# A planned attention order: transfers that share a modelled wire, late tables and weights, half of k loaded, k cast by GpSimd

## The chip, the cores and the metric

The kernel runs on one core of one Trainium2 chip. The metric is the time of one execution on the device in microseconds (us); lower is better. The engines are TensorE (PE; its weight loads are listed as PEld), VectorE (DVE), ScalarE (ACT), GpSimd (POOL) and SyncE (SP, which here only issues transfers).

## What is computed

An attention with 4 x 8 heads of 576 x 64, whose scores carry a bias from a running sum of `s`, and behind it two expert layers over its 2304 rows of 512: a max of three products with an output product, and a routed layer with 8 experts, one chosen per row.

```python
scores = scale * np.matmul(q, k.transpose(0, 1, 3, 2))
cum = np.cumsum(np.maximum(s, 0.0), axis=-1)
bias = -(cum[:, :, :, None] - cum[:, :, None, :])
scores = np.where(causal, -1000000000.0, scores + np.minimum(bias, 0.0))
attn = softmax(scores); x = attn @ v                  # per head
h = np.maximum(np.maximum(x @ w1, x @ w2), x @ w3)    # first layer
x = h @ w_out
e_idx = np.argmax(x @ w_gate + modality_bias[modality_id], axis=1)
out[mask] = gate_w[mask, None] * (np.maximum(x[mask] @ w1[e], 0.0) @ w2[e])
```

## The kernel before

The 32 heads go in 16 pairs; the four pairs of a batch complete its rows of x. Every product is made in float32 out of rounded halves: a high part (`hl`, `xh`, `w_h`) and a low rest (`q_b`, `xl`, `w_l`).

Per head: `load_x` (L338) brings q and k, each held twice over 2 x 64 partitions, as one tile `qk_r` of 128 x 2 x 576. `k_high` (ck, L366) and `q_high` (cq, L369) cast to the high part `hl` on ACT, `k_low` (kl, L376) makes k's rest on DVE, `q_low` (ql, L379) q's rest `q_b` on POOL, and `k_again` (kb, L372) casts k into `k_b` on POOL. Two further rows of `k_b` hold the bias; they come by a transfer from `augk` (first pair, L352) or from `dk` in DRAM (L354). Then six times two matmuls for the scores (L386, L387), six minima on DVE that also write the scores to `e` (L395), five exponentials on ACT (L402), 15 transposes on PE (L407), and their copies to `pt` by ACT or DVE (L412).

Per pair: the sums `r` (ACT L416), their reciprocal (DVE L419), a transpose (PE L423), a copy `r_t` (ACT L427), a transfer to DRAM (`r_d`, SP L430) and two back, spread over 64 partitions each (`rb`, SP L435); the P·V matmuls (L442); and x = P·V times `rb` on DVE (L448, L452). DVE takes its instructions in order, so a late `rb` holds up all that stands behind L448.

Beside the heads run "fills": matmuls of the first expert layer (L240 to L242, 128 x 288, 504 of them) for rows whose pairs are done. They have the lowest priority on PE. Their weights come as 64-bit numbers (`w_raw`, 512 KB, SP L204), are turned by ACT and three DVE steps on `w_z`, sent by a POOL-issued transfer into `w_h` (L225), and POOL makes `w_l` (L229) when that has landed. Nine weight tiles go this way; the other fifteen are converted after the attention, by ACT and DVE.

All of this is one list of jobs (L489 to L550). `planned` (L112) walks through them with a cost per job, a landing time per transfer (`land`), a ring of buffers per kind (`BUFS`) and per engine one queue. At each step it takes, among the jobs that can start soon, the one with the lowest key (`KEY`, per kind, plus `T` for every head). The order so found is the program order of every engine, SP's queue included. Every transfer on SP also waits until the one eight transfers before it has landed. After the attention the order is the framework's.

Of the kernel before, what the change touches and what calls it, by code (L numbers as in the profile page):

```python
# [16 lines left out]
T = B * S  # L17
# [76 lines left out]
class Slot:  # L94

    def __init__(self, pool):
        self.pool, self.users = pool, []


class Job:  # L100

    def __init__(self, run, eng, ns, key, after=(), takes=(), uses=(), land=0, lock=False, ready=0, lag=0):
        self.run, self.eng, self.ns, self.key, self.ready = run, eng, ns, key, ready
        self.after, self.takes, self.land, self.lock, self.lag = list(after), list(takes), land, lock, lag
        self.start = self.end = self.done = None
        for u in [*uses, *takes]:
            if self not in u.users:
                u.users.append(self)


def planned(jobs):
    free, order, then, left, cand = {e: 0 for e in LAT}, {p: [] for p in BUFS}, {}, {}, {e: [] for e in LAT}  # L112
    lock_v = lock_g = 0
    out = []

    def behind(j, a):
        if a.eng == "SP" or a.eng != j.eng:
# [22 lines left out]
    while len(out) < len(jobs):  # L140
# [32 lines left out]
def fused_kernel(tc, qk, vd, sd, w64, mod, wg, wgt, mb, we, cst, csi, out):  # L173
# [3 lines left out]
    with top:  # L177
# [73 lines left out]
        with ExitStack() as es:  # L251
# [237 lines left out]
            for n, h in CONV:  # L489
                raw, z = Slot("raw"), Slot("z")  # L490
                a = job(("wl", n), lambda n=n: w_load(n), "SP", 450, at(h, "wl"), takes=[raw], land=W_NS)
                for k, (what, eng, ns, u, lock, land) in enumerate([("wz", "ACT", 669, [raw], False, 0), ("w1", "DVE", 424, [], False, 0), ("w1", "DVE", 686, [raw], True, 0), ("w1", "DVE", 690, [raw], True, 0), ("wd", "POOL", 570, [], False, 4000), ("ws", "POOL", 1277, [], False, 0)]):
                    a = job(("w", n), lambda n=n, k=k: w_step(n, k), eng, ns, at(h, what, k), after=[a], takes=[z] if k == 0 else [], uses=u + [z], land=land, lock=lock)
            rows = job("rows", rows_out, "SP", 1300, -1e8, ready=8700)
            turns = None
            for h in range(2 * NP):
                p, j = divmod(h, 2)
                s_x, s_k, s_h, s_q, s_e = (Slot(n) for n in ("qk", "kb", "hl", "qb", "e"))
                lx = job(("lx", h), lambda h=h: load_x(h), "SP", (1200, 900, 600)[min(h, 2)], at(h, "lx") if h > 2 else -1e9 + h, takes=[s_x], land=(3400, 3000, X_NS)[min(h, 2)], ready=750)
                lk = job(("lk", h), lambda h=h: load_k(h), "SP", 300 if h > 1 else 450, at(h, "lx", 1) if h > 1 else -2e8 + h, after=[rows] if h > 1 else [], takes=[s_k], land=2000, ready=7800)  # L500
# [21 lines left out]
                if j:  # L522
# [11 lines left out]
                if h % H == H - 1 and NFILL[b]:  # L534
                    for i in range(b * S // FW, (b + 1) * S // FW):
# [501 lines left out]
```

## Time and profile before

| | |
|---|---|
| time, median of 3 runs (lowest, highest) | 761.88 us (756.9, 762.68) |
| the profiled execution: time, span | 761.99 us, 760.2 us |
| PE busy | 715.9 us, 94% |
| PEld busy | 638.2 us, 84% |
| DVE busy | 518.5 us, 68% |
| ACT busy | 407.5 us, 54% |
| POOL busy | 180.9 us, 24% |
| transfers | 108.56 MB, 143 GB/s in the mean |

Busy time is a share over stages with different limits, and a busy PE is not PE at its peak, because the ends of its pipelined matmuls are modelled; the spacing of their starts tells its real pace. The attention takes about the first 242 us of the span, the expert layers the rest. [...] A row's bracket names the idle time of the engine in front of the instruction and what seems to have ended it.

### The profile page before, as it was taken

To read this page: it belongs to the slowest core of one execution; us is meant where nothing else is said; L and a number is where in the kernel's file an instruction comes from. 1 tells how busy PE (TensorE), PEld (TensorE's weight loads), DVE (VectorE), ACT (ScalarE), POOL (GpSimd) and SP (SyncE) were. 2 spreads that over 40 slices of the span, in tenths; PEclk is the share of its full clock that TensorE was granted. 3 is DMA by queue.
4 is the path that set the end of the run, shared out by engine and by line. 5 is a ranking of instruction groups with operands and counts; after the bars stand their busy time and mean duration, and the time that the engine had idled before them with its cause. 6 is when DMAs were issued, how large, how long until landed. Compare 5 with 4: busy or idle time off the path is not lost. (4 is left out here: it accounts for less than half of the span.)

```text
span 760.2 us, 13607 instructions
## 1 busy us (share of the span) xinstructions
PE 715.9 (94%) x4602; PEld 638.2 (84%) x4602; DVE 518.5 (68%) x1567; ACT 407.5 (54%) x992; POOL 180.9 (24%) x202
## 2 busy tenths in 40 slices
PE   1969889999999989999999999998999999999996
PEld 1757678778888989999898998997899888999884
DVE  4869987979777694294676876673786555576540
ACT  5869778887985352221222222444557555575541
POOL 5345645442430220001010101024133122121101
PEclk9989999999999999999999999999999999999999
DMA  6556775754432650011101012567587675756610
GB/s 218 194 162 192 234 207 147 236 147 156 146 88 71 217 168 36 11 43 10 55 10 63 22 48 22 183 192 193 146 196 289 218 241 191 262 209 196 208 68 18
DMA packets 45104, 108.56 MB, mean 143 GB/s; under 512 B 8992, under 2 KB 12992, under 8 KB 45024
## 3 DMA queue, kind: packets, MB, share of 16 engines
q1 hardware_dynamic: 37376, 90.75, 38.7%
q0 software_dynamic: 4912, 11.82, 5.4%
q10 hardware_dynamic: 2736, 5.01, 1.8%
q8 instruction: 38, 0.62, 0.4%
q14 instruction: 42, 0.34, 0.2%
HBM read 93.55 MB, written 12.18 MB: 139 GB/s over the span
## 5 line engine op out<-in xcount | busy, mean ns | idle before, releaser
L240 PE MATMUL a_ps<-xh,w_h 128*128 128x384 f32 (+2 forms) x492 | 160.5, 327 | 3.3 <-ACT h L482 2.2
L241 PE MATMUL a_ps<-xl,w_h 128*128 128x384 f32 (+2 forms) x492 | 157.5, 320 | 1.0 <-POOL xl L471 1.0
L242 PE MATMUL a_ps<-xh,w_l 128*128 128x384 f32 (+2 forms) x492 | 157.3, 320 | 0.2 <-POOL w_l L229 0.2
L739 DVE TENSOR_TENSOR e_l<-e_raw,e_h 128x512 fp32r<-128x512 f32 x160 | 104.2, 686 | 17.6 <-ACT e_h L738 15.9
L738 ACT CAST e_h<-e_raw 128x512 fp32r<-128x512 f32 x160 | 93.3, 622 | 20.2 <-DMA e_raw<-in_we 11.7
L240 PEld LDWEIGHTS a_ps<-xh,w_h 128*128 128x128 f32 x492 | 92.9, 189 | 4.9 <-ACT h L482 2.8
L402 ACT ACTIVATE e<-e,mn 128x448 f32<-128x448 f32 (+4 forms) x160 | 88.7, 556 | 12.2 <-DVE mn L395 12.1
L241 PEld LDWEIGHTS a_ps<-xl,w_h 128*128 128x128 f32 x492 | 93.0, 189 | 2.0 <-POOL xl L471 1.5
L242 PEld LDWEIGHTS a_ps<-xh,w_l 128*128 128x128 f32 x492 | 92.8, 189 | 0.5 <-POOL w_l L229 0.4
L769 PE MATMUL h_ps<-x2t,e_h 128*128 128x256 f32 x288 | 81.0, 282 | 0.0
L770 PE MATMUL h_ps<-x2t,e_l 128*128 128x256 f32 x288 | 80.9, 282 | 0.0
L768 PE MATMUL h_ps<-x2t,e_h 128*128 128x256 f32 x288 | 80.5, 282 | 0.0
L647 POOL DMA_INDIRECT table<-meta,si x18 | 19.7, 1093 | 248.5 <-DVE nm L635 70.5
L407 PE MATMUL t_ps<-ident,e 128*128 128x128 f32 x480 | 73.1, 285 | 5.5 <-DVE x L452 3.2
L622 DVE CUSTOM_DVE_ANT_0 junk<-x,wg 128x512 bf16<-128x512 f32 x96 | 65.9, 686 | 17.2 <-ACT x L700 16.2
L386 PE MATMUL s_ps<-hl 128*128 128x288 f32 (+1 forms) x192 | 64.9, 348 | 12.4 <-DVE hl L376 10.2
L395 DVE CUSTOM_DVE_ANT_0 e<-s_ps,mask 128x288 f32<-128x288 f32 (+4 forms) x160 | 63.7, 425 | 10.5 <-PE s_ps L387 9.9
L407 PEld LDWEIGHTS t_ps<-ident,e 128*128 128x128 f32 x480 | 55.8, 144 | 11.4 <-DVE x L452 4.3
L387 PE MATMUL s_ps<-k_b,q_b 66*128 66x288 f32 (+1 forms) x192 | 58.5, 318 | 5.3 <-POOL q_b L379 5.3
L798 PE MATMUL y_ps<-e_h,gh 128*128 128x512 f32 x152 | 61.5, 405 | 0.4 <-ACT gh L790 0.4
L800 PE MATMUL y_ps<-e_h,gl 128*128 128x512 f32 x152 | 60.7, 399 | 0.0
L799 PE MATMUL y_ps<-e_l,gh 128*128 128x512 f32 x152 | 60.0, 395 | 0.0
(177 smaller groups left out, 1466.1 us busy)
## 6 DMA issues: line engine op xcount, KB each, us to landing
e_raw<-in_we SPq DMA_DIRECT2D x80, 512.0 KB
qk_r<-in_qk SPq DMA_DIRECT2D x30, 576.0 KB
w_raw<-in_w SPq DMA_DIRECT2D x24, 512.0 KB
v_r<-in_vd SPq DMA_DIRECT2D x16, 320.0 KB
rb<-r_d SPq DMA_DIRECT2D x32, 160.0 KB
x2d<-x ACTq DMA_DIRECT2D x18, 256.0 KB
w_h<-w_z POOLq DMA_DIRECT2D x9, 256.0 KB, 7.2
wg<-in_wg SPq DMA_DIRECT2D x4, 512.0 KB
```

The source lines that it names most:

```text
L240: P.matmul(a_ps, wh[:, c], xh[:, c], start=c == 0, stop=False)
L241: P.matmul(a_ps, wh[:, c], xl[:, c], start=False, stop=False)
L242: P.matmul(a_ps, wl[:, c], xh[:, c], start=False, stop=c == 3)
L386: P.matmul(s_ps, hl[:, 1, q0:q0 + 128], hl[:, 0, k0:k0 + n], start=True, stop=False)
L402: A.activation(out=ec, in_=ec, func=ACTF.Exp, bias=tl["mn", h][:, c:c + 1], scale=-1.0, accum_out=tl["l", p][:, j, c:c + 1])
L407: P.transpose(out=t_ps[:, n * 128:(n + 1) * 128], in_=e_bufs[h % E_N][:, EOFF[c] + kb * 128:EOFF[c] + (kb + 1) * 128], identity=ident)
L622: V.tensor_tensor_reduce(out=junk, in0=x2, in1=wg_sb[ei // 2][:, ei % 2, :], scale=1.0, scalar=0.0, op0=ALU.mult, op1=ALU.add, accum_out=l ...
L738: A.copy(out=h, in_=raw[:, a])
L739: V.tensor_tensor(out=lo, in0=raw[:, a], in1=h.bitcast(F32), op=ALU.subtract)
L768: P.matmul(h_ps, w(hs, f, c), xt[:, 0, c], start=c == 0, stop=False)
L769: P.matmul(h_ps, w(hs, f, c), xt[:, 1, c], start=False, stop=False)
L770: P.matmul(h_ps, w(ls, f, c), xt[:, 0, c], start=False, stop=c == 3)
```

## The change

`CK` moves the cast of k's high part from ACT to POOL. `load_x` loads of k only partitions 64 to 127 (144 KB instead of 288) and q apart (288 KB), so two issues a head; `k_again` reads k from there. The planner gets a `wire`: transfers take their bytes' time one behind the other, 1.3 us after their issue at the earliest, and land 0.9 us later; before, each landed by a time of its own. The transfers of the tables for the routing may not start before 150 us of the plan, the weights' not before 15 us, and the landing of `w_h` is put at 3.5 us instead of 4.0. All numbers of `KEY` are new. The work of the engines is otherwise the same.

```diff
-CK = "ACT"
+CK = "POOL"
-W_NS, X_NS, SET_H = 6500, 4500, 24
-KEY = {"T": 6784, "wl": 43955, "wz": 15084, "w1": -2025, ...}
+W_READY, SET_H = 15000, 24
+WIRE_FROM, WIRE_TO, WIRE_SLOW = 1300, 900, 1.0
+KEY = {"T": 6868, "wl": 10316, "wz": -156821, "w1": 25206, ...}
...
-        return a.end + a.land + j.lag
+        return (a.done if a.wire or a.land else a.end) + j.lag
...
         j.done = j.end + j.land + TAIL.get(j.eng, 0)
+        if j.wire:
+            wire = max(wire, t + WIRE_FROM) + j.wire * WIRE_SLOW
+            j.done = max(j.done, wire + WIRE_TO)
...
-                if p == 0:
-                    for t in range(2):
-                        (SP, A)[t if j == 0 else 0].dma_start(out=x[:, 1 - t], in_=qk[PORD[p], :, 1 - t, j])
-                else:
-                    SP.dma_start(out=x, in_=qk[PORD[p], :, :, j])
+                SP.dma_start(out=x[64:128, 1], in_=qk[PORD[p], 64:128, 1, j])
+                (SP if h else A).dma_start(out=x[:, 0], in_=qk[PORD[p], :, 0, j])
...
-                G.tensor_copy(out=tl["k_b", h][0:64], in_=tl["x", h][0:64, 1])
+                G.tensor_copy(out=tl["k_b", h][0:64], in_=tl["x", h][64:128, 1])
...
-                a = job(("wl", n), lambda n=n: w_load(n), "SP", 450, at(h, "wl"), takes=[raw], land=W_NS)
+                a = job(("wl", n), lambda n=n: w_load(n), "SP", 450, at(h, "wl"), takes=[raw], wire=1500, ready=W_READY)
...
-                    rr = job(("rr", p), lambda p=p: r_in(p), "SP", 1100, at(h, "rw", 1), after=[a], takes=[s_r], land=2200)
+                    rr = job(("rr", p), lambda p=p: r_in(p), "SP", 1100, at(h, "rw", 1), after=[a], takes=[s_r], wire=1700)
...
-            job("tables_in", t_in, "SP", 2800, at(SET_H, "lx", 2))
+            job("tables_in", t_in, "SP", 2800, at(SET_H, "lx", 2), ready=150000, land=3000)
```

The line numbers of the changed kernel are higher by one from L343 on (by four around L204 to L229).

The start of the program on SP, before: ahead of these rows stand the load of `s`, two of `v_r`, one of `qk_r` (head 0's k) and the mask.

```order
L346 DMA ident<-in_cst 128x128
L341 DMA qk_r<-in_qk 128x576 x2
L343 DMA qk_r<-in_qk 128x2x576
L204 DMA w_raw<-in_w 128x1024 x2
L304 DMA tri_f<-in_cst 128x128
L305 DMA off<-in_cst 128x8
L306 DMA iota<-in_cst 128x64
L307 DMA table<-sent 128x324
L308 DMA tok<-in_csi 128x18
L309 DMA mod_i<-in_mod 128x36
L310 DMA mb_sb<-in_mb 128x16
L352 DMA k_b<-augk 2x1x576 x2
```

And with the change, from the load of `s` on (L343 is half of k, L344 is q):

```order
L260 DMA s_85<-in_sd 32x576
L343 DMA qk_r<-in_qk 64x576
L346 DMA mask<-in_cst 128x128
L347 DMA ident<-in_cst 128x128
L343 DMA qk_r<-in_qk 64x576
L344 DMA qk_r<-in_qk 128x576
L343 DMA qk_r<-in_qk 64x576
L344 DMA qk_r<-in_qk 128x576
L363 DMA v_r<-in_vd 128x640 x2
L353 DMA k_b<-augk 2x1x576 x2
```

The seven tables and the two weights have left the place in front of `k_b<-augk`, and `v_r` stands behind the heads' loads.

POOL's first work on heads, before:

```order
L379 TENSOR_TENSOR q_b_129<-qk_r,hl 64x576
L372 CAST k_b<-qk_r 64x576
L379 TENSOR_TENSOR q_b_130<-qk_r,hl 64x576
L372 CAST k_b<-qk_r 64x576
L379 TENSOR_TENSOR q_b_131<-qk_r,hl 64x576
```

And with the change (L367 is the cast of k's high part, L380 `q_low`, L373 `k_again`):

```order
L367 CAST hl<-qk_r 64x576 x3
L380 ISA
L380 TENSOR_TENSOR q_b_129<-qk_r,hl 64x576
L373 CAST k_b<-qk_r 64x576 x2
L380 TENSOR_TENSOR q_b_130<-qk_r,hl 64x576
```

Three casts for heads 0 to 2 now stand in front of head 0's `q_b`.

SP around the first pair's `r_d` and `rb`, before:

```order
L343 DMA qk_r<-in_qk 128x2x576
L362 DMA v_r<-in_vd 128x640
L430 DMA r_d<-r_t 10x128
L354 DMA k_b<-dk 2x576
L204 DMA w_raw<-in_w 128x1024 x2
L435 DMA rb<-r_d 64x640 x2
```

And with the change:

```order
L343 DMA qk_r<-in_qk 64x576
L344 DMA qk_r<-in_qk 128x576
L431 DMA r_d<-r_t 10x128
L355 DMA k_b<-dk 2x576
L436 DMA rb<-r_d 64x640 x2
```

The two loads of `w_raw` no longer lie between the two; they stand six rows further up.

POOL around the conversion of weights, before (the third tile):

```order
L225 DMA w_h<-w_z 128x512
L379 TENSOR_TENSOR q_b_129<-qk_r,hl 64x576
L471 TENSOR_TENSOR xl<-x_503,xh 128x288
L372 CAST k_b<-qk_r 64x576
L379 TENSOR_TENSOR q_b_130<-qk_r,hl 64x576
L229 TENSOR_TENSOR w_l<-w_z,w_h 128x512
L372 CAST k_b<-qk_r 64x576
```

And with the change, around the second tile:

```order
L229 DMA w_h<-w_z 128x512
L380 TENSOR_TENSOR q_b_129<-qk_r,hl 64x576
L367 CAST hl<-qk_r 64x576
L233 TENSOR_TENSOR w_l<-w_z,w_h 128x512
L373 CAST k_b<-qk_r 64x576
L472 TENSOR_TENSOR xl<-x_484,xh 128x288
L380 TENSOR_TENSOR q_b_130<-qk_r,hl 64x576
L367 CAST hl<-qk_r 64x576
```

There is less work between the transfer and `w_l`, and casts of k stand on both sides of it.

## Rows read from the trace of the kernel before

**Rows 1.** Stages: stretch, us; busy us of PE, PEld, DVE, ACT, POOL; PEclk, DMA share, GB/s.

```profile
0.00:16.00 16.00, 0.58 (x1) 0.29 (x1) 6.39 (x9) 8.93 (x13) 9.15 (x35) 1.00 0.76 249
16.00:37.60 21.60, 19.98 (x112) 16.27 (x112) 17.53 (x65) 17.30 (x53) 7.71 (x10) 1.00 0.54 170
37.60:44.60 7.00, 0.25 (x3) 0.08 (x2) 2.05 (x5) 2.14 (x6) 3.06 (x3) 0.76 1.15 304
44.60:48.40 3.80, 3.80 (x19) 3.71 (x20) 2.44 (x12) 2.72 (x9) 2.76 (x3) 0.55 0.17 58
48.40:103.00 54.60, 51.47 (x393) 41.62 (x391) 50.09 (x142) 46.48 (x130) 26.71 (x27) 1.00 0.64 197
103.00:156.00 53.00, 49.59 (x364) 40.85 (x363) 42.42 (x135) 41.98 (x119) 27.80 (x29) 0.97 0.64 185
156.00:239.60 83.60, 83.13 (x656) 71.25 (x655) 66.95 (x233) 69.20 (x201) 26.31 (x26) 1.00 0.41 124
239.60:300.00 60.40, 56.05 (x368) 53.02 (x368) 44.73 (x79) 24.73 (x49) 8.34 (x8) 1.00 0.44 146
300.00:760.00 460.00, 451.02 (x2700) 411.14 (x2698) 285.94 (x893) 194.05 (x419) 69.08 (x66) 0.99 0.42 128
```

**Rows 2.** Timeline of the start: start us, us, engine, line, operation, tile [idle before].

```profile
6.69 0.74 DVE L262 TENSOR_TENSOR augk<-s,augk 32x576 fp32r<-32x576 f32 x1 [0.74 <-ACT augk L261]
...
7.96 1.24 ACT L366 CAST hl<-qk_r 64x576 fp32r<-64x576 f32 x2 [1.30 <-DMA qk_r<-in_qk]
...
9.98 1.39 POOL L379 TENSOR_TENSOR q_b<-qk_r,hl 64x576 fp32r<-64x576 f32 x1 [6.25 <-ACT hl L369]
...
14.12 1.39 SPq L352 DMA_DIRECT2D k_b<-augk  x2
...
16.09 0.58 PE L387 MATMUL s_ps<-k_b,q_b 66*128 66x288 f32 x1 [5.28 <-POOL q_b L379]
```

**Rows 3.** Transfers of the first 40 us, GB/s in slices of 1 us.

```profile
GB/s 0 41 224 401 348 337 392 353 302 375 263 369 358 189 32 5 28 115 14 18 101 408 410 389 406 46 0 0 0 8 0 0 88 371 395 303 328 406 395 213
```

**Rows 4.** Timeline of SP around the first pair's rb.

```profile
32.51 0.29 SPq L430 DMA_DIRECT2D r_d<-r_t  x1
...
33.19 0.83 SPq L204 DMA_DIRECT2D w_raw<-in_w  x2
36.44 1.14 SPq L435 DMA_DIRECT2D rb<-r_d  x2
```

**Rows 5.** Timelines of DVE and PE: three waits for rb and what followed.

```profile
43.69 0.69 DVE L448 TENSOR_TENSOR x<-o_ps,rb 128x512 f32<-128x512 f32 x1 [4.95 <-DMA rb<-r_d]
...
44.56 0.38 PE L423 MATMUL t_ps<-ident,r 128*10 128x128 f32 x1 [6.75 <-DVE r L419]
...
110.52 0.69 DVE L448 TENSOR_TENSOR x<-o_ps,rb 128x512 f32<-128x512 f32 x1 [2.44 <-DMA rb<-r_d]
...
200.08 0.69 DVE L448 TENSOR_TENSOR x<-o_ps,rb 128x512 f32<-128x512 f32 x1 [1.88 <-DMA rb<-r_d]
```

**Rows 6.** Groups by shape, 16 to 240 us: count, busy us, mean ns, idle before.

```profile
L366 ACT CAST hl<-qk_r 64x576 fp32r<-64x576 f32 x29 | 19.4, 669 | 1.4 <-PE s_ps L386 0.7
...
L376 DVE TENSOR_TENSOR hl<-qk_r,hl 64x576 fp32r<-64x576 f32 x29 | 26.2, 905 | 3.3 <-ACT hl L366 2.6
...
L379 POOL TENSOR_TENSOR q_b<-qk_r,hl 64x576 fp32r<-64x576 f32 x30 | 43.6, 1455 | 47.2 <-ACT hl L369 47.0
...
L229 POOL TENSOR_TENSOR w_l<-w_z,w_h 128x512 fp32r<-128x512 f32 x9 | 12.3, 1369 | 16.6 <-DMA w_h<-w_z 16.6
```

**Rows 7.** Line L376 in the whole run: duration ns min/median/max.

```profile
L376 DVE TENSOR_TENSOR hl<-qk_r,hl x32: 751/754/1828, 8.7 to 218.6; 64x576 fp32r<-64x576 f32 x32
```

**Rows 8.** Tile w_h up to 240 us: its transfers from issue to landing.

```profile
DMA to landing us min/median/max: 6.3/7.2/7.7
```

**Rows 9.** Timeline of PE in a stretch of fills.

```profile
198.00 0.29 PE L241 MATMUL a_ps<-xl,w_h 128*128 128x288 f32 x1
198.13 0.29 PE L242 MATMUL a_ps<-xh,w_l 128*128 128x288 f32 x1
```

More of the change, by code (lines that the diff above doesn't have):

```diff
@@ L100, with __init__ @@
 class Job:
-    def __init__(self, run, eng, ns, key, after=(), takes=(), uses=(), land=0, lock=False, ready=0, lag=0):
+    def __init__(self, run, eng, ns, key, after=(), takes=(), uses=(), land=0, lock=False, ready=0, lag=0, wire=0):
         self.run, self.eng, self.ns, self.key, self.ready = run, eng, ns, key, ready
-        self.after, self.takes, self.land, self.lock, self.lag = list(after), list(takes), land, lock, lag
+        self.after, self.takes, self.land, self.lock, self.lag, self.wire = list(after), list(takes), land, lock, lag, wire
         self.start = self.end = self.done = None
@@ L112, in planned @@
     free, order, then, left, cand = {e: 0 for e in LAT}, {p: [] for p in BUFS}, {}, {}, {e: [] for e in LAT}
-    lock_v = lock_g = 0
+    lock_v = lock_g = wire = 0
     out = []
@@ L490, in fused_kernel @@
                 raw, z = Slot("raw"), Slot("z")
-                a = job(("wl", n), lambda n=n: w_load(n), "SP", 450, at(h, "wl"), takes=[raw], land=W_NS)
-                for k, (what, eng, ns, u, lock, land) in enumerate([("wz", "ACT", 669, [raw], False, 0), ("w1", "DVE", 424, [], False, 0), ("w1", "DVE", 686, [raw], True, 0), ("w1", "DVE", 690, [raw], True, 0), ("wd", "POOL", 570, [], False, 4000), ("ws", "POOL", 1277, [], False, 0)]):
+                a = job(("wl", n), lambda n=n: w_load(n), "SP", 450, at(h, "wl"), takes=[raw], wire=1500, ready=W_READY)
+                for k, (what, eng, ns, u, lock, land) in enumerate([("wz", "ACT", 669, [raw], False, 0), ("w1", "DVE", 424, [], False, 0), ("w1", "DVE", 686, [raw], True, 0), ("w1", "DVE", 690, [raw], True, 0), ("wd", "POOL", 570, [], False, 3500), ("ws", "POOL", 1277, [], False, 0)]):
                     a = job(("w", n), lambda n=n, k=k: w_step(n, k), eng, ns, at(h, what, k), after=[a], takes=[z] if k == 0 else [], uses=u + [z], land=land, lock=lock)
-            rows = job("rows", rows_out, "SP", 1300, -1e8, ready=8700)
+            rows = job("rows", rows_out, "SP", 1300, -1e8, ready=8700, wire=300)
             turns = None
@@ L498, in fused_kernel @@
                 s_x, s_k, s_h, s_q, s_e = (Slot(n) for n in ("qk", "kb", "hl", "qb", "e"))
-                lx = job(("lx", h), lambda h=h: load_x(h), "SP", (1200, 900, 600)[min(h, 2)], at(h, "lx") if h > 2 else -1e9 + h, takes=[s_x], land=(3400, 3000, X_NS)[min(h, 2)], ready=750)
-                lk = job(("lk", h), lambda h=h: load_k(h), "SP", 300 if h > 1 else 450, at(h, "lx", 1) if h > 1 else -2e8 + h, after=[rows] if h > 1 else [], takes=[s_k], land=2000, ready=7800)
+                lx = job(("lx", h), lambda h=h: load_x(h), "SP", 1300 if h == 0 else 900, at(h, "lx") if h > 2 else -1e9 + h, takes=[s_x], ready=750, wire=1700)
+                lk = job(("lk", h), lambda h=h: load_k(h), "SP", 300 if h > 1 else 450, at(h, "lx", 1) if h > 1 else -2e8 + h, after=[rows] if h > 1 else [], takes=[s_k], wire=100, ready=7800)
                 if j == 0:
                     s_v, s_p, done = Slot("vr"), [], []
-                    lv = job(("lv", p), lambda p=p: values_in(p), "SP", 430, at(h, "lv") if p else -9e8, takes=[s_v], land=3000)
+                    lv = job(("lv", p), lambda p=p: values_in(p), "SP", 430, at(h, "lv") if p else -9e8, takes=[s_v], wire=1300, ready=2000)
                 ck = job(("ck", h), lambda h=h: k_high(h), CK if h else "ACT", 671, at(h, "ck"), after=[lx], takes=[s_h], uses=[s_x], ready=0 if h else 6640)
```

6 lines of the change are left out of this document (3 added, 3 removed).

## The prediction

> **What bounds the kernel now.** I read the table of stages first [rows 1]. From 156 us on TensorE (PE) is busy without a gap: 83.1 of 83.6 us up to 239.6, 451.0 of 460 after 300. The time after the attention is PE's own work, the change leaves its instructions as they are (a few neighbours swap places), and it can only begin sooner. [...] Because PE is full later on, a microsecond that it gets back early comes off the end, as long as no other engine takes it: VectorE (DVE) is busy 50.1 of 54.6 us from 48.4 to 103 and is the next bound.
>
> The profiled execution is 761.99 us (span 760.2 and 1.8 around it); the median of the runs shown is 761.88. The sum is made against 761.99. About 1% (7.6 us) is what a measurement of this kernel can tell from no change.
>
> **The start.** The first scores take two matmuls; the second, with k_b and q_b, runs at 16.09 us [rows 2]. The row names q_b as the releaser, but that was written by 9.98 + 1.39 = 11.37. What came last is the two rows of augk in k_b: they were complete on DVE at 6.69 + 0.74 = 7.43, and SP issued them at 14.12, behind w_raw and the seven loads of the tables. From that issue to the matmul passed 1.97 us. In the changed order nothing but loads for the first heads stands ahead of them, so they are issued near 7.5 and there by 9.6. Then GpSimd (POOL) is last. By its order it casts k of heads 0, 1 and 2 first (k_high goes by CK alone, so head 0's cast is there too, though the planner books it on ACT), then subtracts q_b of head 0, then casts k_b. The third cast needs head 2's k. In the old order 1288 KB lay on the wire up to head 0's k (s 72, q 288, two v_r 640, k 288); by the slices these had passed at about 5.9 us [rows 3] and the cast began at 7.96, 2.05 later [rows 2]. In the new order it is 1208 KB up to head 2's k, so it is there near 7.7. Cast 0.67, q_b 1.46 (mean), k_b about 0.67 [rows 6]: PE's second matmul at 10.5. **Gain 5.6 us.** Bounds: 6.5 if k_b's rows decide, 3.5 if the loads arrive 2 us later. The conversions of weights that ACT and DVE did in this hole come later, inside DVE's and ACT's work: 2 x 0.67 us of ACT, paid by the casts that ACT loses.
>
> Half of k is not loaded: 144 of 576 KB a head. I give that no gain of its own, since after 156 us the wire's share is 0.41 and earlier 0.54 to 0.64 [rows 1]. In the one stretch where rb's loads of 64 partitions make up much of the traffic, 37.6 to 44.6, 304 GB/s go with a share of 1.15, 264 GB/s for a full share; in the first 16 us, with loads of 128 partitions, it is 249 / 0.76 = 328 [rows 1]. So narrow loads seem dearer per byte. [...]
>
> **The first rb.** r_d of the first pair is issued at 32.51, two w_raw (1 MB) at 33.19, rb at 36.44 [rows 4]; DVE waits 4.95 us for rb in front of x at 43.69, the reciprocal of the next pair stands behind x in DVE's order, and PE waits 6.75 us for that [rows 5]. Price: 7.0 − 0.25 = 6.75 idle and 3.8 x 0.45 = 1.7 of slow clock, 8.4. In the new order w_raw stands well ahead of r_d and only k_b's row lies between r_d and rb, and in DVE's order the work between the pair's reciprocal and its x is as long as before (about 8 us by the durations). What wait remains I take as 0.5; the bound is 1.88, the wait where no w_raw lay between (200.08) [rows 5]. **Gain 7.9**, between 6.5 and 8.4.
>
> **Later waits.** DVE waits 2.44 us for the sixth pair's rb at 110.5 [rows 5], which also had a w_raw ahead of it; PE stops, and the granted clock of the stage is 0.97 in the mean, worth 53 x 0.03 = 1.6 [rows 1]. With the 3.4 idle of this stage at most 5.0 can go. In the new order a w_raw lies between r_d and rb only for pair 11, late, where PE has fill to do; but for six pairs (2, 6, 9, 10, 12, 13) a head's two loads lie there, 432 KB. I take **3.5**, between 0 and 5.0.
>
> **k cast by POOL.** 32 casts of 0.67 us leave ACT, 21.4 us [rows 6]. ACT is busy 46.5 of 54.6 us where DVE has 50.1 [rows 1], so it seldom ends a wait there: **1.0**, between 0 and 3.1 (PE's idle of that stretch). POOL grows from 94 busy us between 16 and 239.6 (the six stages of [rows 1]) to 116 and stays the emptiest engine. k_again reads partitions 64 to 127 and writes 0 to 63, which POOL does nowhere now; DVE's L376 crosses the same way at 751 ns against ACT's 669 for the same tile, so I take no extra time; twice the length would be 21 us more on POOL, which has over 80 free.
> The casts can also hinder DVE. kl (L376) takes 905 ns in the mean, 751 at best [rows 6, 7]: 29 x 0.154 = 4.5 us with 94 us of POOL beside it, so 21.4 us more add 1.0. **Loss 1.0**; the other bound is every cast in front of a kl, 29 x 0.67 = 19.4. [...]
>
> **The rest.** Seven table loads go to about 150 us of the plan, where their SP time is hidden by three buffers of q and k; they cost a late load, if that cover fails. Thirty-one more issues of about 0.5 us are hidden in SP's waits. Fills move later: 297 of their 504 matmuls stand ahead of the last P·V matmuls now, 252 then. The 45 of 0.13 us [rows 9] are 6 us that go behind, in a stretch where PE is nearly full either way, so they cost nothing and lengthen the cover for the weights' conversion; of PE's 4.35 idle us from 239.6 to 300 I take **1.0** back (0 to 4.35).
>
> Sum: −5.6 − 7.9 − 3.5 − 1.0 + 1.0 − 1.0 = −18.0; 761.99 − 18.0 = **744**.
>
> **Rivals.**
> *All holes close.* −6.5 − 8.4 − 5.0 − 3.1 − 4.35 = −27.35, 734.6 us. For it: the plan now books transfers behind each other, and rb's own time with 3.9 us from issue to landing instead of 3.3. Against it: DVE at 92% is next.
> *The rb wait moves.* The six pairs with a head's loads between r_d and rb wait as the sixth does now: 6 x 2.44 = 14.6 given back, 758.6 us. For it: the wire's slices stand at 300 to 400 GB/s whenever several loads are out [rows 3]. Against: 432 KB is less than half of what delayed the first pair.
> *POOL stops and DVE with it: slower.* w_h goes out through POOL's queue and takes 7.2 us to land [rows 8]; the plan gives it 0.57 + 3.5. w_l waits for it on POOL, 16.6 us over 7 times now [rows 6], with q_b and k_b behind; now k's casts stand behind it too, and kl, which DVE meets in order. In the new order 2.1 to 3.5 us of POOL work lies between w_h and w_l, so each of nine waits some 3 us; if DVE and then PE stop, each also leaves about 1.7 of slow clock, 4.7 together. Six of nine (28 us) outweigh the 18 by 1%: 772 us; all nine 786. Against: PE never waited for POOL's q_b or k_b after the first head, and the order of DVE leaves time: counted with the trace's durations from the last step on w_z to the kl of the next cast, one of these has about 1 to 2 us in hand, the others 5.7 or more.
> *The change doesn't get through.* If DVE holds the pace, the start is given back in the attention: only −7.9, 754, the edge of no change. And if every cast met a kl, the bound above, it is 744 − 1.0 + 19.4 = 762; against it, kl is stretched by 0.15 us in the mean now, beside 94 us of POOL.
>
> **Chances.** Forecast 0.50; all holes 0.20; the rb wait moves, the start is given back or the casts meet kl 0.20; POOL 0.10. Faster by over 1% (under 754.4) 0.72: the first two and a little of the third; within 1% 0.18; slower 0.10. The range leaves out POOL's case and a piece at each end: 731 to 759.
>
> **What would show it.** Right: the second matmul of the scores at 9.6 to 12 us; no DVE wait for rb over 2 us and no low clock ahead of 60 us; the last P·V matmuls near 215 to 222 us instead of 239.6, with PE full from there. Wrong: PE waits on POOL's q_b or k_b or DVE on POOL's hl; a low clock elsewhere; PE idle behind the last P·V.

## The result: 1.1% faster, about half of the forecast

| | before | after |
|---|---|---|
| median of 10 runs (lowest, highest) | 761.18 us (756.35, 762.68) | 751.38 us (747.82, 754.4) |
| ratio, with 95% interval | | 0.9888 [0.9858, 0.9917] |
| the profiled execution: time, span | 761.99 us, 760.2 us | 751.17 us, 749.4 us |

The ratio is worth 8.5 us, the two profiled executions differ by 10.8. The forecast was 18.0 off 761.99. The time lies in the range (731 to 759), the direction was right, and the size was off by about half. One execution of a kernel below (land7, 1934.55 us) is left out of every ratio.

The stages of the changed kernel, to be held against [rows 1]. Columns as there: stretch, us; busy us of PE, PEld, DVE, ACT, POOL; PEclk (the granted TensorE clock, as a share of full speed), DMA share, GB/s.

```profile
0.00:12.50 12.50, 0.58 (x1) 0.29 (x1) 8.14 (x8) 5.69 (x8) 8.91 (x35) 1.00 0.68 188
12.50:29.60 17.10, 15.44 (x78) 13.18 (x78) 13.91 (x52) 12.87 (x41) 10.74 (x13) 1.00 0.56 168
29.60:48.00 18.40, 18.15 (x136) 13.59 (x137) 17.85 (x62) 16.39 (x51) 12.34 (x13) 1.00 0.64 186
48.00:60.00 12.00, 10.08 (x63) 7.06 (x62) 9.15 (x26) 7.17 (x24) 5.89 (x7) 0.86 0.70 190
60.00:152.00 92.00, 88.83 (x688) 74.54 (x688) 85.35 (x260) 68.88 (x207) 56.98 (x61) 1.00 0.64 185
152.00:163.50 11.50, 8.56 (x43) 7.95 (x42) 7.20 (x24) 7.75 (x25) 7.97 (x9) 0.70 0.50 153
163.50:227.00 63.50, 61.81 (x492) 52.45 (x492) 50.45 (x170) 44.54 (x136) 19.72 (x21) 1.00 0.33 98
227.00:290.00 63.00, 59.74 (x393) 55.87 (x394) 47.29 (x81) 26.62 (x53) 12.93 (x12) 1.00 0.45 145
290.00:749.00 459.00, 452.57 (x2719) 413.38 (x2717) 286.36 (x894) 194.13 (x420) 68.17 (x66) 1.00 0.39 128
```

The long hole at 37.6 to 48.4 us is gone: from 29.6 to 48 PE works 18.15 of 18.40 us. But two stretches are new. At 48 to 60 PE idles 1.92 us and the granted clock is 0.86 in the mean, worth 12 x 0.14 = 1.7; at 152 to 163.5, where PE idled 0.44 us at full clock in the kernel before, it idles 2.94 and the clock is 0.70, worth 11.5 x 0.30 = 3.45. Together they come to 10.0 us. Up to the last P·V the granted clock is 0.98 in the mean in both kernels, so no slow clock was saved on balance.

The ends of the attention, as PE's rows of the last P·V, before and after:

```profile
239.55 2.69 PE L442 MATMUL o_ps<-pt,v_r 128*64 128x512 f32 x16
...
226.90 2.81 PE L443 MATMUL o_ps<-pt,v_r 128*64 128x512 f32 x20
```

12.65 us earlier. The forecast was −17.0 by the terms ahead of it and −6 for the fills that now stand behind it, 216.6: the attention ended 10.3 us later than forecast. Behind it the kernel takes 522.5 us instead of 520.65, 1.85 more, although 45 fill matmuls more stand there (5.9 us). So 4.0 us came back there, and they have a place of their own. In the kernel before, PE waited once in the routed layer for gathered rows of x (`xg`):

```profile
519.24 2.08 PE L751 MATMUL x_ps<-ident,xg 128*128 128x128 f32 x8 [2.33 <-DMA xg<-x2d,mt]
```

The four microseconds from 519 on ran at a granted 0.57, worth 1.7 more. The changed kernel has no such wait. All three kernels with early tables and weights have one of 2.1 to 2.4 us there (before, b_rb1, b_r3), and of the thirteen with late ones only z3 has one, of 0.7; why is not shown.

**The second of the new holes** shows how they come about. Timelines of POOL, ACT, DVE and PE around 146 to 158 us (start, us, engine, line, operation, tile, idle before):

```profile
145.98 0.56 POOL L229 DMA_DIRECT2D w_h<-w_z  x1 [2.95 <-DVE w_z L226]
...
147.32 1.42 POOL L380 TENSOR_TENSOR q_b<-qk_r,hl 64x576 fp32r<-64x576 f32 x1
153.14 1.26 POOL L233 TENSOR_TENSOR w_l<-w_z,w_h 128x512 fp32r<-128x512 f32 x1 [4.40 <-DMA qk_r<-in_qk]
...
154.44 0.67 ACT L220 ACTIVATE w_z<-w_raw 128x512 f32<-128x512 f32 x1 [5.04 <-POOL w_l L233]
...
155.13 0.43 DVE L222 TENSOR_SCALAR w_z<-w_z 128x512 int32<-128x512 int32 x1 [2.79 <-ACT w_z L220]
...
155.58 0.55 PE L408 MATMUL t_ps<-ident,e 128*128 128x128 f32 x3 [2.03 <-ACT pt L413]
...
157.03 0.37 PE L424 MATMUL t_ps<-ident,r 128*10 128x128 f32 x1 [0.91 <-DVE r L420]
```

POOL issues `w_h` at 145.98. The plan books its landing 0.57 + 3.5 = 4.07 us later; `w_l` starts 7.16 us later, with 4.40 us of waiting in front (the row names a load of qk as its releaser, but what `w_l` reads is `w_h`). `w_l` is the last reader of its `w_z` buffer, and there are two of these. ACT's next `w_z` needs that buffer. The new KEY gives `w_z` the lowest number of all (−156821), which is the highest priority, so it stands at the head of ACT's order and waits there 5.04 us, with an exponential, copies of `pt` and the sums behind it. DVE waits 2.79 us for it, PE 2.03 and 0.91, and the granted clock is 0.54 from 156 to 160 us and 0.60 from 160 to 164. In the whole attention ACT waits 10.9 us for `w_l`, five times; in the kernel before it never did. At 48 to 60 us ACT waits 2.45 in the same way. There PE's 1.92 idle us are two waits: 1.03 behind ACT, and 0.89 for `w_l` itself, in front of a fill:

```profile
51.80 0.40 PE L246 MATMUL a_ps<-xh,w_l 128*128 128x288 f32 x1 [0.89 <-POOL w_l L233]
```

**The first pair's sums and rb**, which answer [rows 4, 5]: reciprocal and x on DVE, `r_d` and `rb` on SP, P·V on PE; then two rows of the kernel before.

```profile
23.42 0.22 DVE L420 RECIPROCAL r<-r 128x10 f32<-128x10 f32 x1
...
25.69 0.31 SPq L431 DMA_DIRECT2D r_d<-r_t  x1
...
28.35 1.10 SPq L436 DMA_DIRECT2D rb<-r_d  x2
...
29.60 2.81 PE L443 MATMUL o_ps<-pt,v_r 128*64 128x512 f32 x20 [0.84 <-ACT pt L413]
...
33.29 0.68 DVE L449 TENSOR_TENSOR x<-o_ps,rb 128x512 f32<-128x512 f32 x1
```

```profile
29.06 2.81 PE L442 MATMUL o_ps<-pt,v_r 128*64 128x512 f32 x20 [0.69 <-ACT pt L412]
...
31.38 0.21 DVE L419 RECIPROCAL r<-r 128x10 f32<-128x10 f32 x1
```

x waits for nothing now. But the reciprocal also stands 6.2 us ahead of the P·V of its pair, where it stood 2.3 us behind it. I had not compared these two in the kernel before.

**The start**, which answers [rows 2]: POOL, SP and PE.

```profile
6.53 2.94 POOL L367 CAST hl<-qk_r 64x576 fp32r<-64x576 f32 x3 [2.81 <-DMA qk_r<-in_qk]
9.57 1.77 POOL L380 TENSOR_TENSOR q_b<-qk_r,hl 64x576 fp32r<-64x576 f32 x1
11.40 1.70 POOL L373 CAST k_b<-qk_r 64x576 fp32r<-64x576 f32 x2
...
7.83 1.41 SPq L353 DMA_DIRECT2D k_b<-augk  x2
...
12.54 0.61 PE L388 MATMUL s_ps<-k_b,q_b 66*128 66x288 f32 x1 [1.73 <-POOL k_b L373]
```

The second matmul comes at 12.54 instead of 16.09, 3.55 us earlier, released by POOL's `k_b` as forecast, but 2.0 later than forecast. The three casts take 0.66, 1.19 and 1.11 us with no gap between them, q_b 1.77, and head 0's `k_b` 1.08 of the 1.70 (the other is head 1's). Beside them DVE makes kl of the first three heads, at 1.11, 1.22 and 1.95 us instead of the 0.75 of its median: side by side both engines take longer (ck_act, below, with no cast of k on POOL, has the three kl at 0.75 and q_b at 1.46).

### The profile page after: what moved, and what is told of

Read it like the earlier page. It is cut to its first block, busy times and chain, and to the rows that moved or that the text cites. A ratio compares the mean times of both kernels' runs of the same rounds, so it can differ in the third digit from the quotient of the medians.

```text
span 749.4 us, 13639 instructions
## 1 busy us (share of the span) xinstructions
PE 715.8 (96%) x4602; PEld 638.3 (85%) x4602; DVE 525.7 (70%) x1567; ACT 384.1 (51%) x960; POOL 203.7 (27%) x234
## 5 line engine op out<-in xcount | busy, mean ns | idle before, releaser
L408 PEld LDWEIGHTS t_ps<-ident,e 128*128 128x128 f32 x480 | 57.0, 144 | 10.8 <-ACT pt L413 4.4
```

What stands on the lines that cost most here:

```text
L408: P.transpose(out=t_ps[:, n * 128:(n + 1) * 128], in_=e_bufs[h % E_N][:, EOFF[c] + kb * 128:EOFF[c] + (kb + 1) * 128], identity=ident)
```

## The experiments

Ratios are to the kernel before, with 95% intervals; a ratio is the better measure, since the medians of before in these comparisons lay between 759.98 and 762.91.

| kernel | median us | ratio |
|---|---|---|
| the change | 751.38 | 0.9888 [0.9858, 0.9917] |
| z3: third w_z buffer | 746.65 | 0.9807 [0.9769, 0.9845] |
| land7: w_h booked at 6.6 | 747.47 | 0.9821 [0.9790, 0.9852] |
| start: casts of heads 1, 2 later | 749.97 | 0.9858 [0.9830, 0.9886] |
| z3_start | 746.98 | 0.9812 [0.9778, 0.9847] |
| land7_start | 746.91 | 0.9792 [0.9744, 0.9839] |
| ck_act: ACT casts k | 752.14 | 0.9893 [0.9850, 0.9936] |
| full_k: whole k loaded | 751.35 | 0.9864 [0.9829, 0.9900] |
| b_rb1: before, rb ahead of w_raw | 759.74 | 0.9988 [0.9962, 1.0013] |
| b_r3: before, sums of 3 pairs earlier | 759.38 | 0.9947 [0.9917, 0.9978] |
| b_late: before, late tables and weights | 769.25 | 1.0108 [1.0071, 1.0145] |
| b_late_key: that with the new KEY | 747.08 | 0.9792 [0.9742, 0.9841] |
| a_oldkey: the change with the old KEY | 767.23 | 1.0046 [1.0017, 1.0076] |
| a_nowire: the change without the wire | 752.26 | 0.9873 [0.9838, 0.9908] |
| key_z3: b_late_key with third buffer | 752.27 | 0.9882 [0.9846, 0.9918] |

### What opened the two holes: z3, land7

z3 gives every third `w_z` of the attention a buffer of its own (the same edit cuts the ring of `r_t` from four to three):

```diff
-            z = zsp.tile([128, 512], F32, name="w_z")
+            z = (z3p[0] if early and k == 2 else zsp).tile([128, 512], F32, name="w_z")
```

> The changed kernel with a third buffer for w_z during the attention (the plan still counts two, so the order of every engine up to the last P.V is the same). Theory ring: POOL's w_l waits for w_h, which lands 5.4 to 7.8 us after its issue where the plan books 4.1; until w_l is through, the w_z buffer is not free, and ACT's next w_z (L220) stands waiting in ACT's queue (10.9 us, 5 times) with exponentials and copies behind it, so PE stops at 48-60 and at 152-163.5 us and its clock falls. Then the wait of ACT for w_l is gone, both stretches run near full clock, and what they cost (idle 1.9 + 2.9, clock 12 x 0.14 + 11.5 x 0.30 = 5.1, 9.9 in all) comes back for the most part: 742 us, 739 to 746. Rival pace: DVE (92% busy) sets the pace of the attention and ACT's wait only shows it; then the holes move and the time stays at 749 to 752.

746.65 us, 0.65 above the range of the first theory. Stages of z3, and the rows behind the place where it still loses time (ACT, DVE, PE):

```profile
48.00:60.00 12.00, 10.34 (x78) 8.03 (x77) 11.34 (x31) 9.56 (x29) 5.72 (x7) 1.00 0.82 210
...
152.00:163.50 11.50, 11.08 (x84) 10.31 (x84) 10.60 (x43) 9.18 (x30) 9.64 (x11) 1.00 0.68 220
```

```profile
134.06 0.66 ACT L220 ACTIVATE w_z<-w_raw 128x512 f32<-128x512 f32 x1 [0.87 <-DMA w_raw<-in_w]
...
134.76 1.52 DVE L222 TENSOR_SCALAR w_z<-w_z 128x512 int32<-128x512 int32 x1 [1.36 <-ACT w_z L220]
...
137.67 0.55 PE L410 MATMUL t_ps<-ident,e 128*128 128x128 f32 x3 [2.13 <-DVE x L455]
```

Both stretches are at full clock, and the later one is all but full (11.08 of 11.50). ACT no longer waits for POOL's `w_l` at all. So the ring of two buffers is shown to be what stopped ACT. The earlier stretch still idles 1.66 us, 0.88 of them for `w_l` in front of the same fill, which a buffer more does not bring earlier. Of the 10 us in the two stretches some 5 come back at the end; part of the rest is a new hole at 135 us: `w_z` now waits for its own load `w_raw`, DVE waits 1.36 for it, and its first step then takes 1.52 us instead of 0.43, beside POOL's `w_l` (134.72 to 135.99).

land7 leaves the two buffers and tells the plan a landing time near the measured one (one entry of the list of steps):

```diff
-("wd", "POOL", 570, [], False, 3500)
+("wd", "POOL", 570, [], False, 6600)
```

> The changed kernel, planned anew with one number changed: w_h is booked to land 6.6 us after its 0.57 on POOL (7.2 in all, as the trace of before had it), not 3.5; two w_z buffers, the same KEY. Theory ring: the plan now knows when w_l gets through and the buffer comes free, and puts ACT's next w_z behind that, so ACT waits for w_l less than 3 us in all and the two holes close without a third buffer: last P.V near 222, 745 to 748 us. Rival pace: the plan's own end of the attention is the same as with 3.5 (last P.V at 208 of the plan against 209), DVE sets the pace, 749 to 753.

747.47 us, last P·V at 219.87; neither ACT nor PE waits for `w_l` anywhere. One number in the plan does what the buffer did: `w_z` of the second hole, for which ACT stood waiting from 149.40, now stands at 157.03 in ACT's order. (The whole order is planned anew by it: 21 fills fewer lie ahead of the last P·V, and DVE waits twice for rb, 1.4 us at most.) Both edits take away the same wait of ACT, and both give 4 to 5 us.

### The start: start, z3_start, land7_start, full_k

start moves two casts on POOL behind head 0's `q_b` and `k_b`; on DVE and SP nothing moves.

```diff
-            sequence = planned(jobs)
+            sequence = early_q(planned(jobs), st)   # ck of heads 1, 2 behind ql, kb of head 0
```

> The changed kernel with POOL's casts of k for heads 1 and 2 behind head 0's q_b and k_b instead of ahead of them; nothing else moves on any engine. Theory early: the start fell short because q_b of head 0 stands behind a cast that waits for head 2's k; now the second matmul comes at 10.5 instead of 12.5 us (ends of bounds 10 and 11), and since PE is full later on, these 2 us come off the end: 749 to 749.5. Rival given back: the scores of heads 1 and 2 come no earlier, and what PE does early it waits for before the first P.V (29.6 us), so the time stays at 751 to 752.

> Both edits in one: the third w_z buffer and POOL's casts of heads 1 and 2 behind head 0's q_b and k_b. If the two gains are apart from each other, 4.7 us of z3 and 2 of the start: 744.5 to 745.5. If the start's is given back, as z3 alone: 746.5.

> The changed kernel, w_h booked to land after 6.6 us as in land7, and POOL's casts of heads 1 and 2 behind head 0's q_b and k_b as in start. If both gains stand apart, 747.5 - 1.4 = 746; if the start's is given back before the first P.V as it was beside the third buffer, 747.5.

PE's second matmul in start:

```profile
10.34 0.58 PE L403 MATMUL s_ps<-k_b,q_b 66*128 66x288 f32 x1 [0.57 <-POOL hl L382]
```

10.34 is where the forecast had the whole change (10.5): what kept the start back is that q_b stands behind two more casts, the last of which ended at 9.47. But the 2.2 us are worth 1.4 by the medians, with intervals that overlap (0.9858 against 0.9888), and nothing measurable beside z3 or land7 (746.98 against 746.65; 746.91 against 747.47). A microsecond at the start is not a microsecond at the end here: of the 2.2 us 1.5 are left at the first P·V (28.11 instead of 29.60).

full_k loads all of k:

```diff
-                SP.dma_start(out=x[64:128, 1], in_=qk[PORD[p], 64:128, 1, j])
+                SP.dma_start(out=x[:, 1], in_=qk[PORD[p], :, 1, j])
```

> The changed kernel with the whole of k loaded again (288 KB over 128 partitions instead of 144 KB over 64), the order of the issues the same. If a load over 64 partitions takes the wire as long as one over 128, nothing changes: second matmul of the scores at 12.5 us, kernel 751 within 2. If the bytes count, head 2's k comes 432 KB later, about 1.3 us at the 330 GB/s of the first microseconds, and the second matmul stands at 13.5 to 14; in the attention 144 KB more a head leave the rest as it is, so 752 to 753.

POOL's third cast in the change, then the third cast, PE's second matmul and the first stretch in full_k:

```profile
8.36 1.11 POOL L367 CAST hl<-qk_r 64x576 fp32r<-64x576 f32 x1
```

```profile
8.58 0.87 POOL L367 CAST hl<-qk_r 64x576 fp32r<-64x576 f32 x1 [0.27 <-DMA qk_r<-in_qk]
...
12.51 0.61 PE L388 MATMUL s_ps<-k_b,q_b 66*128 66x288 f32 x1 [1.73 <-POOL k_b L373]
...
0.00:12.50 12.50, 0.58 (x1) 0.29 (x1) 7.89 (x8) 5.70 (x8) 8.37 (x35) 1.00 0.69 223
```

12.51 against 12.54, with 223 GB/s instead of 188 in the same 12.5 us and the same share of busy DMA engines (0.69, 0.68). With 432 KB more ahead of it head 2's k landed at 8.52 instead of 8.31 (the last landing records of the two traces), where the bytes alone, an estimate by the 328 GB/s of a full share in the first 16 us of the kernel before [rows 1], would have put it 1.3 us later. Loading half of k over 64 partitions brings it 0.2 us earlier, and the second matmul not at all. Why half of the bytes take nearly as long is not shown.

### k cast by POOL: ck_act

```diff
-                (A.copy if CK == "ACT" else G.tensor_copy)(out=hl[64:128, 0], in_=tl["x", h][64:128, 1])
+                A.copy(out=hl[64:128, 0], in_=tl["x", h][64:128, 1])
```

> The changed kernel with k's high cast done by ACT again, at the same place of the list of jobs; the order of all else is the same. Theory ring: the holes at 48-60 and 152-163.5 us stay (w_h lands as late as before), ACT has 20 us more to do in the attention, so 751 us or up to 4 more. Rival casts: POOL's casts stretch kl on DVE (986 ns now, 905 in the kernel before), so kl falls to about 905, DVE gets 2.4 us back and the time falls to 747 to 749. At the start, ACT casts k of heads 0 to 2 after augk, POOL comes to q_b earlier: second matmul at 11 to 12.5 us.

752.14 us, no difference that the intervals tell (some 3 us to either side). kl (DVE) by shape in the attention, in the change and then in ck_act: count, busy us, mean ns, idle before.

```profile
L377 DVE TENSOR_TENSOR hl<-qk_r,hl 64x576 fp32r<-64x576 f32 x29 | 28.4, 986 | 0.8
```

```profile
L377 DVE TENSOR_TENSOR hl<-qk_r,hl 64x576 fp32r<-64x576 f32 x29 | 25.8, 898 | 0.8
```

With the casts on POOL kl takes 88 ns more in the mean, 2.6 us over 29, where the forecast had 1.0; the first step on `w_z` takes 719 instead of 492 ns, 2.5 us more over 11. But neither this nor ACT's work, some 20 us less in the change, reaches the end in this order, nor does the second matmul, which ck_act has at 11.10 us. The rival by which the kernel gets 2 to 4 us back falls; terms of 1 us are too small for these runs.

### What kept rb late: b_rb1, b_r3

b_rb1 swaps, in the kernel before, the first pair's rb with the two w_raw ahead of it in SP's order:

```diff
 L354 DMA k_b<-dk 2x576
-L204 DMA w_raw<-in_w 128x1024 x2
 L435 DMA rb<-r_d 64x640 x2
+L204 DMA w_raw<-in_w 128x1024 x2
```

> The kernel before with one swap in SP's queue: the first pair's two loads of rb ahead of the two loads of w_raw (33.19 and 36.44 us in its trace) instead of behind them. By the prediction's term for the first rb DVE's wait of 4.95 us and PE's of 6.75 us go, and so does the slow clock behind them: 7.9 us off 762, 754, between 753 and 755.5. Rival: part of it comes back later, since w_raw lands 1 to 2 us later and other rb's still wait (1 to 2.4 us each): 757 to 760.

759.74 us, no difference. SP and DVE in b_rb1:

```profile
32.22 0.29 SPq L436 DMA_DIRECT2D r_d<-r_t  x1
...
35.83 2.29 SPq L441 DMA_DIRECT2D rb<-r_d  x2
...
38.21 1.02 SPq L210 DMA_DIRECT2D w_raw<-in_w  x2
...
42.55 0.69 DVE L454 TENSOR_TENSOR x<-o_ps,rb 128x512 f32<-128x512 f32 x1 [4.67 <-DMA rb<-r_d]
```

With nothing between them but a small load, rb is still issued 3.6 us behind `r_d` (3.9 before), and SP issues nothing from 32.80 to 35.83. By the waits of the kernel before, SP stood 2.4 us for `r_d` to land in front of this rb, not behind w_raw. DVE's wait is 4.67 instead of 4.95. My reading of [rows 4] took what stood between two rows for what the second waited on, and that is shown wrong.

b_r3 moves the chain of the sums of pairs 1, 7 and 12 forward to where their last exponential is done, and leaves w_raw where it was:

```diff
-            sequence = planned(jobs)
+            sequence = r_first(planned(jobs), st)   # r1, r2, rt, rc, rw, rr of pairs 0, 6, 11
```

> The kernel before with only the chain of the sums (r on ACT, its reciprocal on DVE, its transpose on PE, r_t on ACT, r_d and rb on SP) of pairs 1, 7 and 12 put forward to where their last exponential is done, 4 to 5 us earlier in the plan. These are the three pairs whose reciprocal stands behind the start of their own P.V (31.38 against 29.06 us, 122.3 against 121.8, 190.5 against 189.9); w_raw stays between r_d and rb. Theory lead: it is the late reciprocal that makes rb late, so DVE's waits of 4.95 and 1.88 us for rb go, PE's hole of 6.75 us with its slow clock closes, and the time falls by the 7.9 of the prediction and 1 to 2 more: 751 to 753. Rival wire: rb is held up by the transfers around it (w_raw, the heads' loads); then DVE's wait at the first pair stays above 3 us and the time at 757 to 761.

759.38 us, −0.5%. DVE and PE in b_r3, and a stage of b_r3 and then of the kernel before:

```profile
27.13 0.22 DVE L454 RECIPROCAL r<-r 128x10 f32<-128x10 f32 x1 [0.49 <-ACT r L451]
...
40.37 0.69 DVE L483 TENSOR_TENSOR x<-o_ps,rb 128x512 f32<-128x512 f32 x1
...
33.19 1.95 DVE L411 TENSOR_TENSOR hl<-qk_r,hl 64x576 fp32r<-64x576 f32 x1
...
35.45 0.40 PE L421 MATMUL s_ps<-hl 128*128 128x288 f32 x1 [2.12 <-DVE mn L430]
...
37.60:48.40 10.80, 9.91 (x46) 9.26 (x46) 7.36 (x26) 7.67 (x26) 6.62 (x8) 0.54 0.71 255
```

```profile
37.60:48.40 10.80, 4.05 (x21) 3.79 (x21) 4.49 (x16) 4.86 (x15) 5.82 (x6) 0.68 0.80 217
```

The theory of the lead is right about the wait: with the reciprocal 2.2 us ahead of its P·V, DVE's wait for the first rb is gone, and so is that of pair 12; those of pairs 6 and 9, which were not moved, stay (1.95 and 2.69 us). It is wrong about the price. PE now works 9.91 of these 10.8 us instead of 4.05, but at a granted 0.54, and it had stood idle just before, 2.12 us for a minimum that lay on DVE behind three steps on `w_z` and a kl of 1.95 us, beside POOL's q_b. The second P·V starts 2.0 us earlier, not 8. Closing a hole uncovered the shortage on DVE beneath it.

### Which part carries the gain: b_late, b_late_key, a_oldkey, a_nowire, key_z3

> The kernel before with one part of the change alone: the tables for the routing not before 150 us of the plan and the weights not before 15 us; its KEY, its landing times, full k and ACT's casts stay. If the gain of the change comes from getting these transfers out of the way, the start (second matmul at 16.1) comes down to 11 to 12.5 us and the first pair's rb no longer waits for w_raw: 762 - 4 - 7 = 751 us, as fast as the whole change. If it takes the wire in the plan and the new KEY, a w_raw or a head's loads come to lie in front of some rb again, and less than half of this appears: 757 to 762.

> The kernel before with late tables and weights and the new KEY, but the old landing times (no wire in the plan), whole k, k cast by ACT. With the old KEY the same late transfers gave 769. Theory lead: in this plan the reciprocals stand 5 to 10 us ahead of their P.V (with the old KEY -2 to 3 in the first pairs), so no DVE wait for rb over 1.5 us is left and the time is near that of the whole change, 749 to 755. Rival wire: without the modelled wire rb is booked 3 us too early at every pair, DVE waits for it as with the old KEY (8.8 us in b_late), 760 to 768.

> The changed kernel with the KEY of before: the wire in the plan, late tables and weights, half of k, POOL's casts stay. Theory lead: in this plan the first pair's reciprocal stands 1.1 us behind its P.V again and those of pairs 4 to 8 only 0.8 to 5 us ahead; the wire puts x further back on DVE, but PE's transposes wait for x's bank instead, so PE stands still as in the kernel before: 758 to 766. Rival wire: the modelled wire is what counts, 750 to 755.

> The change in all its parts but the modelled wire: new KEY, late tables and weights, half of k, POOL's casts, w_h booked at 3.5, every other transfer with its old landing time. If the wire in the plan is what costs the 4 us between b_late_key (747.1) and the change (751.4), this runs at 746 to 748. If half of k and POOL's casts cost them once the order is another (kl stretched by 0.1 us in the mean, POOL's queue longer in front of w_l, so ACT's w_z waits more for its buffer), it runs at 750 to 752, and ACT waits for w_l over 5 us in all, where b_late_key has 2.0.

b_late is the kernel before with the two `ready` times of the change; b_late_key has the new KEY too; a_nowire adds to that half of k, POOL's casts and `w_h` at 3.5; a_oldkey is the change with

```diff
-KEY = {"T": 6868, "wl": 10316, "wz": -156821, "w1": 25206, ...}
+KEY = {"T": 6784, "wl": 43955, "wz": 15084, "w1": -2025, ...}
```

With late transfers in all five kernels, the ratios are:

| | no wire in the plan | wire in the plan |
|---|---|---|
| old KEY | 1.0108 (b_late) | 1.0046 (a_oldkey) |
| new KEY | 0.9792 (b_late_key), 0.9873 (a_nowire) | 0.9888 (the change) |

With late transfers the new numbers of KEY carry all of the gain, and more: without them the other parts make the kernel slower. (No run has the new KEY without late transfers.) The late transfers alone bring the second matmul to 12.94 us, but b_late's time lies above both of its expectations. Up to its last P·V PE idles as long as in the kernel before (31.1 and 30.8 us), and the granted clock is 0.94 in the mean instead of 0.98, worth some 9 us of 246; in a_oldkey it is 0.95, in b_late_key 0.99. DVE in b_late, PE in a_oldkey and in b_late_key (waited for: us in total, times, longest):

```profile
DVE x L448 <- DMA rb<-r_d: 8.8, 6, 2.5
```

```profile
PE s_ps L387 <- DVE mn L396: 12.0, 7, 4.1
```

```profile
PE t_ps L423 <- DVE r L419: 2.6, 4, 1.1
```

With the old KEY DVE waits for rb (no wire), or it waits half as long (4.2 us, 3 times) and PE waits for DVE's minima, up to 4.1 us, where the wire puts x further back. With the new KEY no DVE wait for rb shows in the change and in b_late_key (in a_nowire, land7, land7_start and key_z3 there are two each, of 1.6 us at most): the reciprocals stand 6.2 to 13.3 us ahead of their P·V in the change and 5.4 to 10.4 in b_late_key, by the rows of the 16 pairs. The theory of the lead had both kernels on the right side, 747 below its 749 to 755 and 767 above its 758 to 766. It is shown for the waits of pairs 1 and 12 (b_r3) and fits the others, though a lead of 6.0 us did not spare key_z3 a wait of 1.6; which other numbers of KEY make up the rest of the gain, after b_r3's 0.5%, is open. The modelled wire, which I thought the heart of the change, is worth nothing that these runs show under the new KEY (0.9873 and 0.9888).

What remains is 0.9792 against 0.9873, b_late_key against a_nowire. Half of k and POOL's casts are the parts that differ, yet undone within the change's own order (full_k, ck_act) they cost nothing that shows. Neither case of a_nowire's expectation came out whole: 752.26 us is just above the second, but ACT waits 4.7 us for `w_l`, not over 5, and the second matmul comes at 14.50 us, 1.6 later than in b_late_key. key_z3 tells why I don't ascribe this difference to them:

> b_late_key (new KEY, late tables and weights, no wire, whole k, ACT's casts) with a third w_z buffer at run time. ACT's wait for w_l is 2.0 us there, once, so by the theory of the ring there is little left to win: 745 to 747. If the rest of its hole at 152-163.5 us (PE busy 8.65 of 11.5) comes from that wait, 743 to 745.

752.27 us, far above both expectations: a buffer more, and 0.9% slower. ACT and PE in key_z3:

```profile
139.83 0.66 ACT L216 ACTIVATE w_z<-w_raw 128x512 f32<-128x512 f32 x1 [4.82 <-DMA w_raw<-in_w]
...
142.46 1.12 PE L409 MATMUL t_ps<-ident,e 128*128 128x128 f32 x4 [3.26 <-DVE x L454]
```

With the buffer free earlier, `w_z` waits 4.82 us for its load, issued at 133.47, and PE 3.26. ACT's `w_z` waits 2.0 us for `w_l` and 2.7 for `w_raw` with two buffers (b_late_key), and 7.9 for `w_raw` alone with three (key_z3). So orders that are about equally good differ by 0.8% through one or two such waits, and which part of a plan is to blame for a difference of that size is open.

## Why the prediction was right or wrong

**What bounds the kernel** held: from 163.5 to 227 us PE idles 1.7 of 63.5 us, from 290 on 6.4 of 459, and 6.8 of the 10.8 us are gained ahead of the last P·V (12.65 less the 5.9 of the fills). It failed in one place: behind the last P·V PE did not only do its own work, it waited 2.33 us for `xg` at 519.

**The start, −5.6, measured −3.55**: the lower bound was 3.5. Two steps failed. "It is there near 7.7" for head 2's k: it landed at 8.31, since half of k came only 0.2 us earlier than the whole (8.52 in full_k), and POOL was in its second cast until then; the third began at 8.36. And "cast 0.67, q_b 1.46, k_b about 0.67": they took 1.11, 1.77 and 1.08 beside kl on DVE, 1.2 of the 2.0 us. The prediction charged the casts for hindering kl and put what kl does to POOL at nothing; in ck_act, with no cast of k on POOL, the first three kl take 0.75 us each and q_b 1.46. That the gain would come off the end was also too simple (start).

**The first rb, −7.9**: the wait went, as forecast, and with it the slow clock, 0.55 from 44.6 to 48.4 [rows 1]. The cause given for it, w_raw between r_d and rb, was wrong (b_rb1: 0.9988). It was the late reciprocal; and the wait was not worth 7.9, for with it alone taken away DVE's own queue stops PE in its place (b_r3: 0.9947 with two further pairs).

**Later waits, −3.5**: no DVE wait for rb is left in the attention, as far as the rows tell again by the lead of the reciprocals and not by what lies in SP's queue; no run moved these alone.

**k cast by POOL, −1.0 and +1.0**: nothing that ck_act could show; kl's stretch was mis-sized, 2.6 us instead of 1.0, and hidden.

**The rest, −1.0**: 5.9 us of fills went behind the last P·V and only 1.85 us were added, so about 4.0 came back. That it is near the bound of 4.35 is luck: from 239.6 to 300 us little was won (PE idles 3.26 us of the 60 behind the last P·V instead of 4.35), and the 4.0 are the wait for `xg` with its slow clock, 2.33 and 1.7. They cover part of what was lost ahead, and that the time lies in the range owes something to it.

**What the sum left out** are the two new holes, 10 us by their stretches and about 4 to 5 by the runs that close them (z3, land7); this is the larger part of what is missing. The step that failed is the argument against the rival on POOL: I had named the place (w_h lands after 7.2 us, the plan gives it 0.57 + 3.5) and the length (some 3 us each), and followed it to kl on DVE, where there was time in hand. I did not follow it to the other one who waits for `w_l`: the `w_z` buffer, and through it ACT, whose `w_z` the diff itself puts in front of everything. Nor did I follow it to PE's fills, one of which waits 0.89 us for `w_l`. "PE never waited for POOL's q_b or k_b" said nothing on that. The rival's time of 772 was too high, since five of nine waits reached ACT, two of them PE. The landing of `w_h` took 5.4 to 7.8 us in the changed kernel where the plan has 4.07: a plan is better fed with the measured time.

**A version that beats both**: z3, at 0.9807 [0.9769, 0.9845] of before where the change is at 0.9888 [0.9858, 0.9917]; land7_start and b_late_key do as well (0.9792).

## What to carry to other kernels

When an order is planned, look for the instruction that has been put at the head of an in-order queue, list everything it waits for (its buffer's last reader too), and compare the booked landing of each transfer in that chain with the measured one: one landing time booked 3 us short cost 4 to 5 us here. When something waits for a transfer, ask first how early the chain that feeds it begins, and only then what else lies in the queue; two neighbouring rows of a queue are no proof that one waits for the other. A hole's length, 10.0 us for the two here, was an upper bound of its price, 4 to 5: what lies under it is known only once it is closed.

## What the runs showed of the hardware that was not expected

- A `w_h` transfer of 256 KB, issued by POOL from one SBUF tile to another, lands after 5.4 to 7.8 us in the changed kernel, 5.2 to 9.3 in land7.
- Three loads of 144 KB over 64 partitions instead of 288 KB over 128 brought head 2's k 0.2 us earlier (8.31 and 8.52 us), and the second matmul not at all (12.54 and 12.51).
- With POOL's instructions beside it, DVE's kl took 1.11 to 1.95 us at the start of the change, and POOL's casts, beside kl, up to 1.19; with k cast by ACT (ck_act) the first three kl took 0.75 each.
- DVE's first step on `w_z` (a shift of one SBUF tile by a constant) took 1.52 us beside POOL's `w_l` (z3, 134.76), and 0.43 where it began ahead of POOL's next instruction (the changed kernel, 155.13).
- In b_r3 a wait of 2.12 us, in front of 35.45, was followed by a granted clock of 0.50 from 37.6 to 46 us and 0.67 to 48.4, although PE worked 9.91 of these 10.8 us (one further wait, of 0.89, lay in front of 41.23).
